# PSUM banks of the pairs' pools, the last W2 chunks of a pair, and the sixth row of a batch in a fused attention and ResMLP kernel

## The chip, the cores and the metric

The kernel runs on one core of one Trainium2 chip. The metric is the device time of one execution in microseconds; the time before is the median of three runs. All times inside a profile are counted from the start of the profiled span.

The engines are named as in the profile: PE is TensorE's matmul, PEld its weight load, DVE is VectorE, ACT is ScalarE, POOL is GpSimd, SP is SyncE. POOL and SP issue DMAs here. PSUM has eight banks; a bank holds 512 float32 values on each of 128 partitions, which is what one matmul of this kernel fills at most.

## The reference

```python
# attention: 8 batches, 16 query heads, 4 key/value heads, 384 tokens, head size 64
k = np.repeat(k, group, axis=1); v = np.repeat(v, group, axis=1)
scores = scale * np.matmul(q, k.transpose(0, 1, 3, 2))
attn = softmax(scores)
x = np.matmul(attn, v)             # laid out as [8, 384, 1024]
# ResMLP
a1 = alpha1 * x + beta1
tok = np.einsum('ts,bsd->btd', w_tok, a1)
u = x + lam * tok
a2 = alpha2 * u + beta2
ch = np.maximum(a2 @ w_ch1, 0.0) @ w_ch2    # 1024 -> 4096 -> 1024
out = u + lam * ch
```

Inputs and output are float32; the matmuls are done in bfloat16 with float32 sums.

## The kernel before

**Two streams, interleaved.** For each batch there is a "side" (attention and token mixing: everything up to a2) and a channel MLP. The channel MLP of batches 0 and 1 is done plainly (`main`). Batches 2 to 7 go in three pairs (`pair(i)`, i = 0, 1, 2), each by a scheme of the Strassen-Winograd kind with seven products for two batches. The generator of the channel MLP yields after each small piece of matmul work, and a plan written out by hand (`plan`) says which steps of which side run at which yield. So the order on every engine is fixed by the program text; it follows the order in which the instructions are issued.

**Stage 1 of a pair** has eight steps g = 0 to 7. A step has 14 groups of four matmuls of 384 columns (`SEQ1`, line 720): products o = 1 to 7 for two halves e of 128 hidden units. They are summed into PSUM tiles X (o = 1, 6, 5, 3), Y (o = 7, 4) and Z (o = 2), which ACT and DVE empty. The operands on the activation side are the tiles `opb(0)` to `opb(6)`: the transposed a2 of the two batches and sums of it. `sums_a(j)` (three DVE additions, lines 584 to 586) makes such sums for two rows of a2; one more, `opb(6)`, is made after the fourth group of g = 0 (line 737). `sum_w1(g, o)` makes W1's sums for step g on DVE (lines 619 and 624), and for g + 1 they are made during step g, the first of them (o = 5) after the third group.

**Stage 2 of a pair** has seven products, in the order o = 1, 2, 6, 5, 3, 7, 4 (`PLACE2`). Each has three row blocks ms = 0, 1, 2, and each of these 16 matmuls of 512 columns into a tile C (line 781). The work goes in pieces of four matmuls, called half blocks here, u = 0 to 83: after each the generator yields. The last product, o = 4, is done in two halves h = 0 and 1 with three tiles C open at once: ms = 0 and 1 in the pool "acc", ms = 2 in a tile of the pool "sc". Where a product is done, DVE adds it to an earlier one (line 818, for o = 7 line 820 too), scales it by lam (`scaled`, line 684, called a little later by `flush`), and POOL adds it into `out` in DRAM (`store`, line 515).

**The side in stage 2.** While stage 2 of pair i runs, the sides of both batches of the next pair run between its half blocks, the second 39 half blocks after the first. A batch has eight rows p = 0 to 7 (a row is two heads, 128 columns). For each row: scores and exponentials (`scores3`), then `av` (18 matmuls, line 314), after which DVE computes for this row rinv, xr, a1f and a (lines 319, 322, 327, 329); then `tok_flip`: `tok` (nine matmuls, line 339) with DVE's sum u (line 346) and a2 (line 350), the spill of u to `out` by SP (`spill`), and the transposition of a2. For the last three rows of the second batch this is done by PE (`turn`, three matmuls, line 426, and a copy by ACT), for all others by a DMA transpose on SP's queue. The tables of `side` give the half block of each step; `av` of rows 5, 6, 7 stands at 29, 33, 35, `tok_flip` at 34, 36, 38, `turn` at 37, 39, 41. With the shift by 39 the second batch's end falls into o = 4, whose half blocks are u = 72 to 83.

**PSUM in the pairs.** `share_banks` closes the pools of one stage and opens those of the next. Stage 1 has X (three tiles), Y (three) and Z (two), one bank each, in banks 0 to 2, 3 to 5, 6 and 7. Stage 2 has "sc" (three tiles of two banks each, banks 0 to 5), which serves the scores, av, tok and turn in rotation (`three`) and gives C of ms = 2 of o = 4 its tile, and "acc" (two tiles, banks 6 and 7) for all other C. A new pool over the banks of an old one waits for the old pool's last readers.

**Weights.** `w1` is a ring of six slots of 512 KB, for chunks of W1 (loaded and cast from DRAM on POOL's queue, `load_w1`, line 185) and, in stage 2, for the 28 chunks of W2's combinations (`fetch`, from the DRAM scratch `w2s` on SP's queue, line 635). `pad` has two more such slots; in stage 1 it holds W1's sums. `queue` lists loads in order; `pump` issues the head of it whenever a slot comes free (`free`). A step g of stage 1 needs the chunks g and g + 8, which are `order1[2g]` and `order1[2g+1]`. Four of them, for g = 0 and 1, are loaded ahead in stage 2 of the pair before (`heads`).

Of the kernel before, what the change touches and what calls it, by code (L numbers as in the profile page):

```python
# [12 lines left out]
def kernel(  # L13
# [22 lines left out]
    f32 = mybir.dt.float32  # L36
# [158 lines left out]

    def three():
        if pairs:
            return pairs["sc"].tile([P, 2, 4, P], f32, tag="sc", name="sc", bufs=3)
        return threes[0].tile([P, 2, 4, P], f32, tag="sc", name="sc", bufs=3)

    def one():
# [26 lines left out]
    def side(b):  # L228
# [201 lines left out]
        if not first:  # L430


            turns = {}
            if b == 1:
                turns = {4: [(to_all, 3, 0, 0), (to_all, 3, 1, 1), (load_row_set, 1, 1, 0), (load_row_set, 2, 0, 1)],
                         8: [(k_transpose, 0)], 12: [(to_all, 1, 0, 2), (to_all, 1, 1, 0), (load_row_set, 2, 1, 0)],
                         16: [(scale_beta,)], 20: [(to_all, 2, 0, 1), (to_all, 2, 1, 0)],
                         24: [(q_transpose, 0, 2, "av")], 28: [(k_transpose, 2)]}
                for i in range(3):
                    turns[32 + 4 * i] = [(q_transpose, 2 + 2 * i, 2, "av")]  # L440
            if (b - NPL) // 2 > 0:
                at = {}

                def put(k, *m):
                    at.setdefault(k, []).append(m)

                for j in range(6):
                    put((0, 6, 12, 21, 26, 31)[j], scores3, j, j in (2, 5))
                for p in range(NP):
                    put((4, 10, 14, 18, 24, 29, 33, 35)[p], av, p)  # L450
                    put((8, 15, 17, 22, 27, 34, 36, 38)[p], tok_flip, p)
                    if by_pe(p):
                        put((37, 39, 41)[p - NP + 3], turn, p)
                return turns, at
            return turns, {
                0: [(scores3, 0)], 4: [(av, 0)], 6: [(scores3, 1)], 8: [(tok_flip, 0)], 11: [(av, 1)],
                13: [(scores3, 2, True)], 15: [(av, 2)], 16: [(tok_flip, 1)], 18: [(tok_flip, 2)], 19: [(av, 3)],
                21: [(scores3, 3)], 23: [(tok_flip, 3)], 25: [(av, 4)], 27: [(scores3, 4)], 29: [(tok_flip, 4)],
                31: [(av, 5)], 33: [(scores3, 5, True)], 35: [(av, 6), (tok_flip, 5)], 37: [(av, 7)],
                38: [(tok_flip, 6)], 41: [(tok_flip, 7)],  # L460
                **{39 + 4 * i - i // 2 * 2: [(turn, p)] for i, p in enumerate((5, 6, 7)) if by_pe(p)}}
# [164 lines left out]
    NB = (B - NPL) // 2  # L626
    w2_slots, w2_at = {}, {}

    def padded(i, n):
        return n % 8 > 5 or i + 1 < NB and n >= SLOTS - 2  # L630

    def fetch(i, n):
        w2_slots[i, n] = slot = (pad_free if padded(i, n) else w1_free).pop(0)
        w2_at[i, n] = ring[:, slot] if slot < RING else pad[:, (slot - RING + 1) * 2048:(slot - RING + 2) * 2048]
        nc.sync.dma_start(out=w2_at[i, n], in_=w2s[n])

# [4 lines left out]
    def pump():  # L641
        while queue:
            f, *a = queue[0]
            if not (pad_free if f == fetch and padded(*a) else w1_free):
                return
            queue.pop(0)
            f(*a)
# [1 line left out]
    pad_free = []  # L649
    queue = []  # L650
    for i in range(NB):
        heads = [(load_w1, c) for c in order1[:4]] if i + 1 < NB else []
        queue += [(load_w1, c) for c in order1[4 if i else RING:]] + [(fetch, i, n) for n in range(SLOTS - 2)] + heads[:2]
        queue += [(fetch, i, n) for n in (SLOTS - 2, SLOTS - 1)] + heads[2:]

    IDENT = mybir.ActivationFunctionType.Identity
    SEQ1 = ((1, 0), (1, 1), (7, 0), (6, 0), (6, 1), (7, 1), (5, 0), (5, 1), (2, 0), (3, 0), (3, 1), (2, 1), (4, 0), (4, 1))
# [4 lines left out]

    def share_banks(*names):
        pair_banks.close()
        for name in names:
            pairs[name] = pair_banks.enter_context(tc.psum_pool(name=name, bufs=3))

    def pair(i):
        b0 = NPL + 2 * i
        share_banks("X", "Y", "Z")  # L670

        ends = {}

# [33 lines left out]
        for g in range(NH // 2):  # L707
            X, Y, snap = {}, {}, {}
            for k, (o, e) in enumerate(SEQ1):
                t = 2 * g + e  # L710
                lo, hi = bias1[:, t:t + 1], bias1[:, NH + t:NH + t + 1]
                if o == 1:
                    X[e] = pairs["X"].tile([P, 512], f32, tag="X", name="X", bufs=3)
                if o == 7:
                    Y[e] = pairs["Y"].tile([P, 512], f32, tag="Y", name="Y", bufs=3)
                if o == 2:
                    Z = pairs["Z"].tile([P, 512], f32, tag="Z", name="Z", bufs=2)
                ps = (X[e] if o in (1, 6, 5, 3) else Y[e] if o in (7, 4) else Z)[:, :S]
                for dt in range(NDT // 2):
                    nc.tensor.matmul(out=ps, lhsT=tb[g, o][:, dt, e * P:(e + 1) * P], rhs=opb(LEFT1[o])[:, dt],  # L720
                                     start=(o in (1, 2, 7) and dt == 0), stop=(dt == NDT // 2 - 1), skip_group_check=True)
                if o in (1, 6, 5):
                    q = ((2 if g % 2 else 8) + 2 * (1, 6, 5).index(o) + e) % 12 * S
                    snap[o, e] = snaps[:, q:q + S]
                    nc.scalar.activation(out=snap[o, e], in_=ps, func=IDENT, bias=hi if o == 5 else lo)  # L725
                if o == 5:
                    tt(out=hid[:, t, 1], in0=Y[e][:, :S], in1=snap[5, e], op=ADD)  # L727
                elif o == 2:
                    tt(out=hid[:, t, 0], in0=ps, in1=snap[1, e], op=ADD)
                elif o == 3:  # L730
                    nc.scalar.activation(out=hid[:, t, 4], in_=ps, func=RELU, bias=hi)
                elif o == 4:
                    tt(out=hid[:, t, 2], in0=ps, in1=snap[6, e], op=ADD)
                if (o, e) in ((2, 1), (3, 1)):
                    free(w1_slots.pop(g if o == 2 else g + NCH // 2))
                if k == 3 and g == 0:
                    tt(out=opb(6), in0=opb(4), in1=opb(5), op=SUB)
                if k == 2 and i and g == 0:
                    sum_w1(0, 4)
                if k in (2, 5, 8, 11) and g + 1 < NH // 2:  # L740
                    sum_w1(g + 1, {2: 5, 5: 7, 8: 6, 11: 4}[k])
                ts = slice(2 * g, 2 * g + 2)
                if k == 1 and g:
                    finish(slice(2 * g - 2, 2 * g))
                if (o, e) == (3, 1):
                    nc.scalar.activation(out=hid[:, ts, 1], in_=hid[:, ts, 1], func=RELU)
                if (o, e) == (4, 1):
                    nc.vector.tensor_scalar(out=hid[:, ts, 2], in0=hid[:, ts, 2], scalar1=0.0, scalar2=None,
                                            op0=mybir.AluOpType.max)
                    tt(out=hid[:, ts, 3], in0=hid[:, ts, 2], in1=hid[:, ts, 1], op=ADD)  # L750
                yield 0
        finish(slice(NH - 2, NH))
        share_banks("sc", "acc")
        acc = pairs["acc"]

        def c_banks(ms):
            return [(0, 512, pairs["sc"].tile([P, 2, 512], f32, tag="sc", name="C", bufs=3)[:, 0] if ms == NST - 1 else
                     acc.tile([P, 512], f32, tag="acc", name="C", bufs=2))]

        X = [c_banks(ms) if last else None for ms in range(NST)]  # L760
# [2 lines left out]
        for k, o in enumerate(PLACE2):  # L763
            whole = not last and o != 4
            for h in range(1 if whole else 2):
                for ms in range(NST):
# [2 lines left out]
                    if last and (o, h) in ((6, 1), (7, 0)):  # L769
                        (lift_end if o == 7 else begin_end)(ms)  # L770
                    if last and (o, h, ms) == (7, 0, NST - 1):
                        X[ms] = [(c0, c1, pairs["sc"].tile([P, 2, 512], f32, tag="sc", name="C", bufs=3)[:, 0, :c1 - c0])
                                 for c0, c1 in ((0, 384), (384, 512))]
                    if whole:
                        X[ms] = [(0, 512, acc.tile([P, 512], f32, tag="acc", name="C", bufs=2))]
                    elif not last and h == 0:
                        X[ms] = c_banks(ms)
                    upto = NH if whole else 8 * h + 8
                    for (c0, c1, x), t in ((c, t) for c in X[ms] for t in range(8 * h, upto)):
                        slot, rhs = w2_slots[i, 4 * k + t // 4], w2_at[i, 4 * k + t // 4]  # L780
# [49 lines left out]
    with tc.manual_schedule(engines=order):  # L830
# [162 lines left out]
        for i in range(NB - 1):  # L993
# [6 lines left out]
            for u, f, h in ((10, flip_q, 0), (17, flip_k, 0), (18, flip_q, 2), (28, flip_q, 4), (33, flip_k, 2), (33, flip_q, 6)):  # L1000
                put(ps, 1, u, f, c + 1, h, 2)
            put_all(ps, 1, side(c + 1)[1], lambda u: u + 39)
            for j, u in ((1, 78), (0, 78), (2, 80), (3, 82)):
                put(ps, 1, u, sums_a, j)
        for ps in range(NPL + NB):
            done = [0, 0]
# [7 lines left out]
            if ps == NPL - 1:  # L1014
                side_banks.close()
                mm_banks.close()
                pairs["open"] = True
            for key in [k for k in plan if k[0] == ps]:
                for f, *a in plan.pop(key):
                    f(*a)  # L1020
# [30 lines left out]
```

## Time and profile before

| | |
|---|---|
| runs | 755.1, 755.03, 754.49 us; median 755.03 |
| profiled execution | 752.46 us, its span 750.7 us, mean granted TensorE clock 0.997 |
| pair 0, stage 1 and stage 2 | 243.3 to 316.1, then X of pair 1 at 421.45 |
| pair 1, stage 1 and stage 2 | 421.45 to 496.0, then X of pair 2 at 601.30 |
| pair 2 | 601.30 to the end, 750.7 |

Below are PE's instructions around the end of pair 0's stage 2. The columns are the start, the time from the first start to the last end, engine, line, operation, output and input, the shape of a matmul, and how many run on end. Matmuls are pipelined, so the ends that are given overlap the next start; what a group costs is read from start to start.

```profile
403.62 1.03 PE L781 MATMUL C<-w,arena 128*128 128x512 bf16 x4
404.49 0.71 PE L314 MATMUL sc<-v,es 128*128 128x65 bf16 x18
405.04 1.02 PE L781 MATMUL C<-w,arena 128*128 128x512 bf16 x4
405.90 0.67 PE L339 MATMUL sc<-a,wtokT 128*128 128x128 bf16 x9
406.40 1.03 PE L781 MATMUL C<-w,arena 128*128 128x512 bf16 x3
```

The first line is the first half block of o = 4 (u = 72), the second is `av` of row 6, the fourth is `tok` of row 5. So a half block takes 404.49 - 403.62 = 0.87 us, an `av` 0.55 and a `tok` 0.50.

The DMAs that the change touches, from the page's list of issues (line, queue, count, KB each, median microseconds from issue to landing):

```profile
w<-in_moe_w_ch_dram POOLq DMA_DIRECT2D x68, 512.0 KB, 10.6
w<-w2s SPq DMA_DIRECT2D x62, 512.0 KB, 4.8
pad<-w2s SPq DMA_DIRECT2D x22, 512.0 KB, 8.2
```

### The profile page before, as it was taken

How to read it: one execution, taken by the hardware profiler on the slowest of the kernel's cores; microseconds unless marked ns; L12 is line 12 of the kernel's file. 1: busy time of each engine (PE TensorE's matmuls, PEld its weight loads, DVE VectorE, ACT ScalarE, POOL GpSimd, SP SyncE). 2: the span in 40 equal slices, each digit the busy share in tenths (PEclk: the TensorE clock that was granted, in tenths of full speed). 3: DMA queues.
4: the chain of work that ended last, by engine and by line, in shares of the span. 5: the costliest groups of instructions: out<-in, count | busy, mean ns of one | idle time of the engine just before them, and what ended most of it. 6: DMA issues, size and time to landing. Idle time of an engine off the chain costs nothing.

```text
span 750.7 us, 14462 instructions
## 1 busy us (share of the span) xinstructions
PE 729.8 (97%) x5710; PEld 419.1 (56%) x5769; DVE 521.3 (69%) x1010; ACT 318.7 (42%) x458; POOL 163.4 (22%) x211
## 2 busy tenths in 40 slices
PE   8999999999999999999999799999999899999997
PEld 5866555666555666555555466655555456654444
DVE  8763466578677899759678777748958977762344
ACT  7622431442432666644333366663343266660000
POOL 9434220520001330301023233200002322100011
PEclk9999999999999999999999999999999999999999
DMA  9999999999998999999979999989979998937975
GB/s 190 195 201 201 207 219 187 167 196 199 237 281 233 159 222 201 269 244 225 262 177 208 200 151 172 175 210 207 270 227 184 210 161 113 141 128 238 293 204 104
DMA packets 218018, 151.32 MB, mean 202 GB/s; under 512 B 88661, under 2 KB 197061, under 8 KB 217949
## 3 DMA queue, kind: packets, MB, share of 16 engines
q0 software_dynamic: 120304, 64.60, 65.4%
q1 hardware_dynamic: 97100, 85.39, 41.5%
q8 instruction: 45, 0.74, 0.4%
q10 hardware_dynamic: 544, 0.39, 0.2%
q14 instruction: 25, 0.20, 0.1%
HBM read 154.84 MB, written 38.27 MB: 257 GB/s over the span
## 4 chain that ended last, share of the span: by engine, by line
PE 86%; DVE 9%; DMA 2%; issue 2%; ACT 0%; DVEq 0%
PE C L781 23%; PE X L720 17%; PE h L530 10%; PE ch L568 10%; PE Y L720 8%; PE sc L278 4%; PE Z L720 4%; PE sc L314 3%; PE sc L339 3%; DMA pad<-w2s 1%; DMA ops<-a 1%; DVE xr L322 1%; DVE a1f L327 1%; DVE xr L346 1%; DVE hT L818 1%
## 5 line engine op out<-in xcount | busy, mean ns | idle before, releaser
L287 ACT ACTIVATE es<-sc 128x1024 bf16<-128x1024 f32 x126 | 121.4, 1023 | 163.9 <-PE sc L278 154.4
L781 PE MATMUL C<-w,arena 128*128 128x512 bf16 (+2 forms) x731 | 169.3, 372 | 1.7
L781 PEld LDWEIGHTS <-arena 128*128 128x128 bf16 x1040 | 94.8, 98 | 103.0 <-issue 8.0
L725 ACT ACTIVATE hT<-X,bias 128x384 f32<-128x384 f32 x144 | 83.6, 581 | 68.7 <-PE X L720 60.8
L720 PEld LDWEIGHTS <-w 128*128 128x128 bf16 x768 | 75.2, 98 | 57.2 <-issue 6.9
L185 POOL DMA_DIRECT2D w<-in_moe_w_ch_dram x68 | 61.0, 914 | 136.9 <-PE X L720 82.0
L568 PE MATMUL ch<-arena,hT 128*128 128x512 bf16 x366 | 87.9, 379 | 1.0 <-issue 0.3
L515 POOL DMA_DIRECT2D out_dram<-hT x33 | 28.5, 863 | 263.6 <-DVE hT L684 165.2
L530 PE MATMUL h<-ops,w 128*128 128x384 bf16 (+1 forms) x480 | 83.1, 327 | 0.8 <-DVE hT L541 0.7
L720 PEld LDWEIGHTS <-pad 128*128 128x128 bf16 x576 | 56.7, 98 | 37.9 <-issue 1.0
L720 PE MATMUL X<-ops,w 128*128 128x384 bf16 x384 | 70.6, 327 | 6.1 <-DVE hT L818 5.3
L720 PE MATMUL X<-ops,pad 128*128 128x384 bf16 x384 | 71.0, 328 | 0.0
L781 PE MATMUL C<-pad,arena 128*128 128x512 bf16 (+2 forms) x268 | 63.2, 373 | 2.8 <-DMA pad<-w2s 2.6
L530 PEld LDWEIGHTS <-w 128*128 128x128 bf16 x480 | 45.4, 98 | 30.2 <-issue 2.4
L568 PEld LDWEIGHTS <-hT 128*128 128x128 bf16 x384 | 34.7, 98 | 36.8 <-issue 2.5
L339 PEld LDWEIGHTS <-wtokT 128*128 128x128 bf16 x576 | 37.5, 98 | 13.9 <-DVE a L329 3.0
L314 PEld LDWEIGHTS <-es 128*128 128x128 bf16 x1008 | 38.3, 97 | 12.4
L727 DVE TENSOR_TENSOR arena<-Y,hT 128x384 bf16<-128x384 f32 x48 | 26.7, 557 | 24.1 <-ACT hT L725 21.8
L346 DVE TENSOR_TENSOR xr<-sc,xr 128x384 f32<-128x384 f32 x56 | 30.9, 551 | 18.1 <-PE sc L339 18.1
L278 PE MATMUL sc<-qT,kT 64*128 64x384 bf16 (+2 forms) x576 | 41.5, 271 | 1.6 <-ACT hT L287 0.3
L319 DVE RECIPROCAL rinv<-sc 128x6 f32<-128x6 f32 x56 | 10.7, 191 | 42.8 <-PE sc L314 42.7
L314 PE MATMUL sc<-v,es 128*128 128x65 bf16 x1008 | 39.9, 193 | 0.0
(138 smaller groups left out, 922.8 us busy)
## 6 DMA issues: line engine op xcount, KB each, us to landing
w<-in_moe_w_ch_dram POOLq DMA_DIRECT2D x68, 512.0 KB, 10.6
w<-w2s SPq DMA_DIRECT2D x62, 512.0 KB, 4.8
pad<-w2s SPq DMA_DIRECT2D x22, 512.0 KB, 8.2
out_dram<-xr SPq DMA_DIRECT2D x56, 192.0 KB, 6.8
out_dram<-hT POOLq DMA_DIRECT2D x33, 256.0 KB, 7.7
arena<-in_moe_w_ch_dram POOLq DMA_DIRECT2D x16, 512.0 KB, 20.0
w2s<-arena SPq DMA_DIRECT2D x28, 256.0 KB, 3.8
q_raw<-in_q_dram POOLq DMA_DIRECT2D x28, 192.0 KB, 10.5
```

Of the source, the lines that this page charges most:

```text
L185: nc.gpsimd.dma_start(out=w1[:, w1_slots[c]], in_=w1src[:, :, c * CW * P:(c + 1) * CW * P])
L278: nc.tensor.matmul(out=sc[:, hh, k % 4:k % 4 + n], lhsT=kT[r, 2 * p // G, BLK[hh][sk], :], rhs=qT[r, p, st:st + n, :], start=True, stop=True)
L287: nc.scalar.activation(out=e, in_=sc, func=EXP, scale=scale_qk)
L314: nc.tensor.matmul(out=av[:, hh, sq, :], lhsT=ess[k // 4][:, m % 2, k % 4, :], rhs=vb[:, sk, hk, :], start=(sk == 0), stop=(sk == NST - 1))
L339: nc.tensor.matmul(out=ps[:, tt, :], lhsT=wtokT[:, st, tt * P:(tt + 1) * P], rhs=a1s[p][:, st, :], start=(st == 0), stop=(st == NST - 1 an ...
L346: nc.vector.tensor_tensor(out=u, in0=ps, in1=u, op=ADD)
L515: nc.gpsimd.dma_start(out=at, in_=o, accum_op=ADD)
L530: nc.tensor.matmul(out=ps[:, :n], lhsT=w1[:, w1_slots[c], dt, j * P:(j + 1) * P], rhs=a2T[:, dt, :n], start=(dt == 0), stop=(dt == NDT - 1))
L568: nc.tensor.matmul(out=ps, lhsT=hT[:, nt, ms * P:(ms + 1) * P], rhs=w2[:, row(nt)[0], row(nt)[1], cs], start=(i == 0), stop=(i == NNT - 1))
L720: nc.tensor.matmul(out=ps, lhsT=tb[g, o][:, dt, e * P:(e + 1) * P], rhs=opb(LEFT1[o])[:, dt], start=(o in (1, 2, 7) and dt == 0), stop=(dt ...
L725: nc.scalar.activation(out=snap[o, e], in_=ps, func=IDENT, bias=hi if o == 5 else lo)
L781: nc.tensor.matmul(out=x, lhsT=hid[:, t, LEFT2[o], ms * P:(ms + 1) * P], rhs=rhs[:, t % 4 * 512 + c0:t % 4 * 512 + c1], start=((not last o ...
```

## The change

It has three parts.

*Banks.* Stage 1 opens its pools in the order Z, X, Y: Z gets four tiles (banks 0 to 3), X two (4 and 5), Y two (6 and 7). Stage 2 opens "acc" (banks 0 and 1) and three pools of one two-bank tile each, sc1 (2 and 3), sc0 (4 and 5) and sc2 (6 and 7). `three` takes them in turn by a counter and leaves out sc1 while C of ms = 2 of o = 4 lies there ("held").

*Chunks.* The last two W2 chunks of pairs 0 and 1 (n = 26 and 27) go to ring slots, not to `pad`, and are queued after the two W1 chunks of g = 0. Only these two W1 chunks stand ahead of them; the two of g = 1 come next, as slots come free. `pad_free` is emptied when a pair begins.

*Places.* For batches 4 and up `tok_flip` of row 5 is at half block 32 instead of 34, its `turn` at 36 instead of 37. `sums_a(1)` is at u = 77 and `sums_a(0)` at u = 74, both 78 before.

```diff
     def three():
         if pairs:
-            return pairs["sc"].tile([P, 2, 4, P], f32, tag="sc", name="sc", bufs=3)
+            pairs["turn"] = (pairs["turn"] + 1 + (pairs["turn"] == 0 and pairs["held"])) % 3
+            return pairs["sc%d" % pairs["turn"]].tile([P, 2, 4, P], f32, tag="sc", name="sc", bufs=1)
...
-                    put((8, 15, 17, 22, 27, 34, 36, 38)[p], tok_flip, p)
+                    put((8, 15, 17, 22, 27, 32, 36, 38)[p], tok_flip, p)
                     if by_pe(p):
-                        put((37, 39, 41)[p - NP + 3], turn, p)
+                        put((36, 39, 41)[p - NP + 3], turn, p)
...
-    def padded(i, n):
-        return n % 8 > 5 or i + 1 < NB and n >= SLOTS - 2
+    def padded(n):
+        return n % 8 > 5
...
     for i in range(NB):
-        heads = [(load_w1, c) for c in order1[:4]] if i + 1 < NB else []
-        queue += [(load_w1, c) for c in order1[4 if i else RING:]] + [(fetch, i, n) for n in range(SLOTS - 2)] + heads[:2]
-        queue += [(fetch, i, n) for n in (SLOTS - 2, SLOTS - 1)] + heads[2:]
+        heads = [(load_w1, c) for c in order1[:2]] if i + 1 < NB else []
+        queue += [(load_w1, c) for c in order1[2 if i else RING:]] + [(fetch, i, n) for n in range(SLOTS - 2)] + heads
+        queue += [(fetch, i, n) for n in (SLOTS - 2, SLOTS - 1)]
...
     def share_banks(*names):
         pair_banks.close()
+        pairs["turn"], pairs["held"] = 2, False
         for name in names:
-            pairs[name] = pair_banks.enter_context(tc.psum_pool(name=name, bufs=3))
+            pairs[name] = pair_banks.enter_context(tc.psum_pool(name=name, bufs=2))
 
     def pair(i):
         b0 = NPL + 2 * i
-        share_banks("X", "Y", "Z")
+        share_banks("Z", "X", "Y")
+        pad_free.clear()
...
-                    X[e] = pairs["X"].tile([P, 512], f32, tag="X", name="X", bufs=3)
+                    X[e] = pairs["X"].tile([P, 512], f32, tag="X", name="X", bufs=2)
                 if o == 7:
-                    Y[e] = pairs["Y"].tile([P, 512], f32, tag="Y", name="Y", bufs=3)
+                    Y[e] = pairs["Y"].tile([P, 512], f32, tag="Y", name="Y", bufs=2)
                 if o == 2:
-                    Z = pairs["Z"].tile([P, 512], f32, tag="Z", name="Z", bufs=2)
+                    Z = pairs["Z"].tile([P, 512], f32, tag="Z", name="Z", bufs=4)
...
-        share_banks("sc", "acc")
+        share_banks("acc", "sc1", "sc0", "sc2")
         acc = pairs["acc"]
 
         def c_banks(ms):
-            return [(0, 512, pairs["sc"].tile([P, 2, 512], f32, tag="sc", name="C", bufs=3)[:, 0] if ms == NST - 1 else
+            return [(0, 512, pairs["sc1"].tile([P, 2, 512], f32, tag="sc", name="C", bufs=1)[:, 0] if ms == NST - 1 else
                      acc.tile([P, 512], f32, tag="acc", name="C", bufs=2))]
...
                     elif not last and h == 0:
                         X[ms] = c_banks(ms)
+                        pairs["held"] = ms == NST - 1
...
-            for j, u in ((1, 78), (0, 78), (2, 80), (3, 82)):
+            for j, u in ((1, 77), (0, 74), (2, 80), (3, 82)):
                 put(ps, 1, u, sums_a, j)
```

The lines left out do the same for the last pair's two split C tiles (they take sc0 and sc2) and for the call of `padded`, and set the counter at the end of `main`. The change shifts line numbers: L781 before is L785 after, L720 is L723, L818 is L822, L684 is L687, L346 is L347, L624 is L625.

More of the change, by code (lines that the diff above doesn't have):

```diff
@@ L627 @@
     w2_slots, w2_at = {}, {}
-    def padded(i, n):
-        return n % 8 > 5 or i + 1 < NB and n >= SLOTS - 2
+    def padded(n):
+        return n % 8 > 5
     def fetch(i, n):
-        w2_slots[i, n] = slot = (pad_free if padded(i, n) else w1_free).pop(0)
+        w2_slots[i, n] = slot = (pad_free if padded(n) else w1_free).pop(0)
         w2_at[i, n] = ring[:, slot] if slot < RING else pad[:, (slot - RING + 1) * 2048:(slot - RING + 2) * 2048]
@@ L643, in pump @@
             f, *a = queue[0]
-            if not (pad_free if f == fetch and padded(*a) else w1_free):
+            if not (pad_free if f == fetch and padded(a[1]) else w1_free):
                 return
@@ L771, in pair @@
                     if last and (o, h, ms) == (7, 0, NST - 1):
-                        X[ms] = [(c0, c1, pairs["sc"].tile([P, 2, 512], f32, tag="sc", name="C", bufs=3)[:, 0, :c1 - c0])
-                                 for c0, c1 in ((0, 384), (384, 512))]
+                        X[ms] = [(c0, c1, pairs[sc].tile([P, 2, 512], f32, tag="sc", name="C", bufs=1)[:, 0, :c1 - c0])
+                                 for sc, c0, c1 in (("sc0", 0, 384), ("sc2", 384, 512))]
                     if whole:
@@ L1016 @@
                 mm_banks.close()
-                pairs["open"] = True
+                pairs["turn"] = 0
             for key in [k for k in plan if k[0] == ps]:
```

## The prediction

> **What bounds the kernel now.** I read the engines' shares, then TensorE's waits, then stretches by stage, then the timelines of TensorE (PE) and VectorE (DVE) in the last microseconds before a pair's stage 1. Times are in the 750.7 us span; the profiled execution took 752.46 us.
>
> ```profile
> PE 729.8 (97%) x5710; PEld 419.1 (56%) x5769; DVE 521.3 (69%) x1010; ACT 318.7 (42%) x458; POOL 163.4 (22%) x211
> ```
> ```profile
> PE X L720 <- DVE hT L818: 5.3, 2, 3.1
> PE C L781 <- DMA pad<-w2s: 2.6, 3, 1.8
> ...
> PE X L720 <- DVE obuf L575: 0.8, 1, 0.8
> ```
> PE is busy 97%, and the change adds or removes no instruction, so only PE's waits can move. Those of the pairs, 5.3 + 2.6 + 0.8 us (total, times, longest), are all this change can reach. They lie at three places: 0.8 where pair 0 begins, the rest where stage 2 of pairs 0 and 1 gives way to the next pair's stage 1.
>
> ```profile
> 414.53 1.89 PE L781 MATMUL C<-pad,arena 128*128 128x512 bf16 x8 [1.76 <-DMA pad<-w2s]
> ...
> 421.45 1.83 PE L720 MATMUL X<-ops,w 128*128 128x384 bf16 x8 [2.28 <-DVE hT L818]
> ```
> ```profile
> 601.30 1.46 PE L720 MATMUL X<-ops,w 128*128 128x384 bf16 x8 [3.06 <-DVE hT L818]
> ```
> So a transition has 1.76 + 2.28 us of idle (pair 0) or about 0.8 + 3.06 (pair 1). Start to start it is 17.83 us in both from the last half block of o=7 (403.62) to X (421.45); its work is 12 C half blocks of 0.864, three tok of 0.50, two av of 0.55, three turns of 0.165 (steps between starts) = 13.46, so 4.37 us is lost.
>
> ```profile
> 421.40:424.90 3.50, 3.45 (x14) 1.82 (x15) 3.31 (x5) 1.16 (x2) 1.63 (x2) 0.64 1.45 198
> ...
> 601.20:604.70 3.50, 3.40 (x21) 2.08 (x22) 3.35 (x5) 1.74 (x3) 0.84 (x1) 1.00 1.42 195
> ```
> The column after POOL's is the granted clock. After pair 0's transition PE ran part of this stretch at half clock and did 14 matmuls; after pair 1's, at 1.00, it did 21. From X to the first Z it took 428.33 - 421.45 = 6.88 us against 5.20: 1.68 us lost.
>
> **The change, part by part.**
>
> *X in other banks.* Before, X's pool begins in bank 0 and its release is pool-wide: it waits for the sum L818 of C of ms=2, which lies in a two-bank tile reaching into X's banks. After, X has banks 4 and 5; their last readers are older, so X follows the last C at once. At pair 0's start X likewise no longer waits for L575: -0.78 us; Y's sums there (L586, ending 244.15) are then needed near 244.3.
>
> *The wait that this makes.* C of ms=2 now takes bank 2, which tok of row 6 used in the half block before it. So it waits for DVE's L346 of that row. What is ahead of it there, from these rows:
>
> ```profile
> 408.57 0.19 DVE L319 RECIPROCAL rinv<-sc 128x6 f32<-128x6 f32 x1
> 408.80 0.56 DVE L322 TENSOR_TENSOR xr<-sc,rinv 128x384 f32<-128x384 f32 x1
> 409.39 0.56 DVE L327 TENSOR_TENSOR a1f<-xr,vecs 128x384 f32<-128x384 f32 x1
> 409.98 0.56 DVE L329 TENSOR_TENSOR a<-a1f,vecs 128x384 bf16<-128x384 f32 x1
> 410.46 0.55 DVE L346 TENSOR_TENSOR xr<-sc,xr 128x384 f32<-128x384 f32 x1
> ...
> 419.69 0.35 DVE L584 TENSOR_TENSOR ops<-ops 128x384 bf16<-128x384 bf16 x1
> 420.08 0.36 DVE L585 TENSOR_TENSOR ops<-ops 128x384 bf16<-128x384 bf16 x1
> 420.36 0.35 DVE L586 TENSOR_TENSOR ops<-ops 128x384 bf16<-128x384 bf16 x1
> 420.62 0.68 DVE L818 TENSOR_TENSOR hT<-C,hT 128x512 f32<-128x512 f32 x1
> ```
> Steps by starts: 0.22, 0.59, 0.59, 0.48 for a row's four; 0.59 for L346 and 0.47 for L350; 0.39 + 0.28 + 0.26 = 0.93 for a sums_a; 0.60 for L818, 0.72 with L684 behind it. PE after: C 403.62, av6 404.99, C, av7 407.27, C to 408.69, turn 5, tok6 408.85 to 409.35. DVE after: o=7's two sums and L684 from 403.82, with tok5's L346 and L350 between (row 5 is now earlier), then row 6's four, row 7's four from 408.1 (av7 ends 407.8), then sums_a(0), moved to this half block, at 410.46, and L346 of row 6 from 411.40 to 411.95. C of ms=2 starts at about 412.08: **2.73 us of idle where there was none.**
>
> *Then.* C of ms=2 to 413.81, tok7 to 414.31, h=1 of ms 0 and 1 with two turns to 418.08, ms=2 to 419.81; X at 419.81, not 421.45. What is late next is DVE: still two sums_a, three L818 and three L684 plus W1's first sum (L624, 0.60). The last L586 ends near 421.9; (7,0), third group of stage 1, needs it for its fourth matmul at 421.6: 0.44 us idle. Loss after: 2.73 + 0.44 = 3.17 against 4.37: **-1.2 us a transition, -2.4 for both.**
>
> *Two chunks into the ring.* The pad wait (1.76; about 0.8) goes. The two fetches issue at 400.6 to 402 when chunks 20 and 21 are read, not at 402.1 to 403.8. W1 of g=1 no longer loads beside them. They are read at 414.3 and 415.2. The fetch that PE waited for was issued at 402.1 and there at 414.5: 12.4 us, with the W1 loads beside it. By that slow row they land at 413.0 to 414.4, by the median of `pad<-w2s`, 8.2 us, at 408.8 to 410.2: cost 0 by either; were they 14 us on their way, 0.8.
>
> *W1 of g=1 later.* Its two loads used to issue at 402.14 and 403.05; now POOL waits with them until chunks 24 and 25 are read, about 413.4 and 414.3. Behind them in POOL's queue stand out_dram stores, which hold up nothing near. DVE's L624 of g=1, due at 424.0, waits for both; behind it is L737, needed by PE at 426.1 and ending 425.55. So a landing up to 424.45 is free. Landings took 5.9 and 8.5 us at 430.7 (two loads, queue otherwise idle), but 16.0 to 18.7 at 402 and 15.1 to 16.7 at 410.5 (four loads beside two fetches). I take the first pair, nearest in load: landing at 419.3 to 422.8, cost 0. The other end: 428.5 to 433, cost 4 to 8.5 a transition. W1 of g=2 is used eight us later and has room by either.
>
> *Y with two banks instead of three.* It then waits for L733 of the g before; by timeline the room is 13 ns at 262.6 and 289.9, 136 ns at 308.1, over 0.4 elsewhere. Cost 0 to 0.3, taken 0.15. X has 1.7 us of room.
>
> *Row 5 sooner.* Its spill and transpose pass flips of q and k in SP's queue, which have some 25 us of room: 0.
>
> *The clock.* Half clock came after 2.28 us of idle (pair 0), not after 3.06 (pair 1). The new 2.73 us stands between them, at both transitions. I assume one halving in two, as before: 0; bounds -1.7 (none) and +1.7 (both).
>
> The Trainium skill ("TensorE: Matmul & The Clock Gate", "Why this matters for your kernels") asks for no idle gaps over about 3 us, one idle window of 3.4 us bringing half clock. By it neither new gap would throttle, and the sum would be 1.7 us better. The trace's halving after 2.28 us says a shorter gap can do it, so I don't take this.
>
> **Sum:** -0.78 - 2.4 + 0.15 = -3.0 us: the profiled execution would take 749.4. The median of the runs, 755.03, is 2.6 us above it; I put the difference on the median: **752.0 us**.
>
> **The rivals.**
> - *More (no halving):* -3.0 - 1.7 = -4.7, 750.3; 748.6 if the timed runs had two before. For it: pair 1's gap of 3.06 did nothing. Against: the 2.28.
> - *Nothing to be measured:* halving in both, -1.3, and a row-6 wait longer by 0.5 each, -0.3: 753.7 to 754.7. For it: DVE, busy 17.1 of the 17.8 us, is the same before and after, so PE may only wait at another place.
> - *Slower (W1 of g=1 late):* DVE stops at L624, and PE at (3,0). It decides from a landing at 424.45 + 1.5 + 0.75 = 426.7, some 12.4 us after issue (1.5 us is the gain of a transition, 0.75 half the bound below). At 16 us it is 430.3, +5.85 a transition: -3.0 + 11.7, 763.7. For it: the rows at 402 and 410; against: those at 430.
> - *It doesn't do what it says:* if X's release still reached the sum of ms=2 (422.09 to 422.77 after, by the chain above), X would start at 422.85, 3.04 us after the last C; with the 2.73 that is 5.77 lost against 4.37: -0.78 + 2 x 1.4 + 0.15 = +2.2, 757.2. The new pools are separate, which speaks against it.
>
> **How the numbers follow.** Forecast 0.45, more 0.17, nothing 0.23, W1 late 0.12, not as it says 0.03. A measurement can tell 0.2%, 1.5 us: faster is under 753.5, slower over 756.5. The forecast and "more" are faster (0.62), "nothing" is same (0.23), the last two are slower (0.15). The range runs from 748.5 (no halving left, two before) to 757 (W1 landing 12.6 us after issue); beyond it lies most of the last two cases, some 0.12; the forecast's own range is 751 to 753.5.
>
> **What would show it.** Right: X L720 no longer follows L818 or L575; no wait for pad; C L781 (now L785) waits 2.7 us for xr L346 (L347) twice; Y waits about 0.4 for sums_a. Wrong: X or Y waiting for w, a C wait over 3.5, L624 held by a DMA, or granted clock 0.64 in both windows after X.

## The result and the profile after

The changed kernel takes 748.1 us (median of six runs, 746.87 to 750.17) against 754.76 for the kernel before beside it: ratio 0.9916, 95% interval 0.9896 to 0.9935. The profiled execution has a span of 745.6 us (747.4 us in all). The forecast was 752.0 with a range from 748.5 to 757: the sign was right, the gain, 6.7 us, is more than twice the 3.0 of the forecast, and the time lies just under the range.

PE's waits from pair 0's start to the last transition, in the changed kernel (total, times, longest):

```profile
PE C L785 <- DVE xr L347: 5.0, 2, 2.5
PE Y L723 <- DVE ops L586: 0.4, 2, 0.2
```

These two are all that is left. Gone are X's waits for L818 (5.3) and for the obuf sum L575 (0.8) and the wait for pad (2.6), as the prediction said. Gone too is one that it left out of its list. In the whole kernel before, the waits also had this line:

```profile
PE sc L339 <- DVE a L329: 1.2, 2, 0.6
```

Two waits of 0.6 us, one in each of pairs 0 and 1. The place is in the middle of stage 2, not at the transition; here is pair 0 before, PE and then DVE:

```profile
363.62 0.68 PE L339 MATMUL sc<-a,wtokT 128*128 128x128 bf16 x9 [0.60 <-DVE a L329]
```
```profile
359.94 0.55 DVE L346 TENSOR_TENSOR xr<-sc,xr 128x384 f32<-128x384 f32 x1
360.53 0.56 DVE L350 TENSOR_TENSOR obuf<-xr,vecs 128x384 bf16<-128x384 f32 x1
361.00 0.68 DVE L813 TENSOR_TENSOR hT<-C,hT 128x512 f32<-128x512 f32 x1
361.61 0.18 DVE L319 RECIPROCAL rinv<-sc 128x6 f32<-128x6 f32 x1
...
363.01 0.56 DVE L329 TENSOR_TENSOR a<-a1f,vecs 128x384 bf16<-128x384 f32 x1
```

This is the first batch of the next pair. DVE works without a gap: row 5's L346 and L350 (the first two lines), a C sum, then row 7's four operations, whose last ends 0.05 us before PE's tok of row 7 starts. With row 5 two half blocks sooner, DVE is done with it earlier and the wait is gone.

The transition of pair 0 in the changed kernel, PE:

```profile
403.57 0.67 PE L340 MATMUL sc<-a,wtokT 128*128 128x128 bf16 x9
...
408.80 0.67 PE L340 MATMUL sc<-a,wtokT 128*128 128x128 bf16 x9
411.94 1.89 PE L785 MATMUL C<-w,arena 128*128 128x512 bf16 x8 [2.48 <-DVE xr L347]
...
419.68 1.46 PE L723 MATMUL X<-ops,w 128*128 128x384 bf16 x8
420.98 0.65 PE L723 MATMUL Y<-ops,w 128*128 128x384 bf16 x3
421.82 0.32 PE L723 MATMUL Y<-ops,w 128*128 128x384 bf16 x1 [0.19 <-DVE ops L586]
```

The first line is tok of row 5, at the end of o = 7; the second is tok of row 6, whose bank C of ms = 2 takes next and waits for: 2.48 us (2.73 was forecast, with the start at 412.08). X follows the last C at 419.68 (419.81 forecast) with no wait. The fourth matmul of (7, 0) waits 0.19 (0.44 forecast). From the end of o = 7 to X it is now 419.68 - 403.57 = 16.11 us, against 17.83.

DVE's row that PE waits for, and what stands ahead of it:

```profile
410.40 0.35 DVE L585 TENSOR_TENSOR ops<-ops 128x384 bf16<-128x384 bf16 x1
410.79 0.36 DVE L586 TENSOR_TENSOR ops<-ops 128x384 bf16<-128x384 bf16 x1
411.07 0.35 DVE L587 TENSOR_TENSOR ops<-ops 128x384 bf16<-128x384 bf16 x1
411.34 0.55 DVE L347 TENSOR_TENSOR xr<-sc,xr 128x384 f32<-128x384 f32 x1
```

The clock after this wait, and in pair 1, in this execution (the column after POOL's is the granted clock):

```profile
411.90:415.40 3.50, 3.41 (x24) 1.93 (x25) 2.16 (x4) 0.00 (x1) 1.83 (x2) 1.00 0.31 65
588.10:591.60 3.50, 3.37 (x24) 1.93 (x25) 2.14 (x5) 0.00 (x0) 1.82 (x2) 1.00 0.98 231
```

Full clock at both. So the execution that was profiled has neither halving; the other runs, below, differ.

### The profile page after: what moved, and what is told of

The parts are those of the page before. It is cut to its first block, busy times and chain, and to the rows that moved or that the text cites. A ratio compares the mean times of both kernels' runs of the same rounds, so it can differ in the third digit from the quotient of the medians.

```text
span 745.6 us, 14462 instructions
## 1 busy us (share of the span) xinstructions
PE 728.5 (98%) x5710; PEld 418.7 (56%) x5769; DVE 522.2 (70%) x1010; ACT 319.1 (43%) x458; POOL 163.2 (22%) x211
## 4 chain that ended last, share of the span: by engine, by line
PE 85%; DVE 7%; DMA 4%; issue 2%; POOL 1%; ACT 0%; DVEq 0%
PE C L785 25%; PE X L723 16%; PE ch L569 10%; PE h L531 10%; PE Y L723 8%; PE sc L279 4%; PE Z L723 4%; PE sc L315 3%; PE sc L340 3%; DMA q_raw<-in_q_dram 2%; DMA ops<-a 1%; DVE xr L323 1%; DVE a1f L328 1%; DVE xr L347 1%; DVE hT L822 1%
## 5 line engine op out<-in xcount | busy, mean ns | idle before, releaser
L785 PE MATMUL C<-w,arena 128*128 128x512 bf16 (+2 forms) x777 | 179.8, 373 | 6.8 <-DVE xr L347 5.0
L785 PEld LDWEIGHTS <-arena 128*128 128x128 bf16 x1040 | 94.8, 98 | 105.7 <-issue 10.3
L723 PEld LDWEIGHTS <-w 128*128 128x128 bf16 x768 | 75.2, 98 | 50.0
L723 PEld LDWEIGHTS <-pad 128*128 128x128 bf16 x576 | 56.3, 98 | 38.0 <-issue 0.8
L723 PE MATMUL X<-ops,w 128*128 128x384 bf16 x384 | 70.3, 326 | 0.0
L723 PE MATMUL X<-ops,pad 128*128 128x384 bf16 x384 | 70.3, 326 | 0.0
L785 PE MATMUL C<-pad,arena 128*128 128x512 bf16 (+2 forms) x222 | 52.0, 372 | 0.1
L347 DVE TENSOR_TENSOR xr<-sc,xr 128x384 f32<-128x384 f32 x56 | 30.9, 552 | 21.3 <-PE sc L340 21.3
L723 PE MATMUL Y<-ops,w 128*128 128x384 bf16 x192 | 39.4, 326 | 0.4 <-DVE ops L586 0.4
L320 DVE RECIPROCAL rinv<-sc 128x6 f32<-128x6 f32 x56 | 10.7, 191 | 40.6 <-PE sc L315 40.5
```

Of the source, the lines that this page charges most:

```text
L347: nc.vector.tensor_tensor(out=u, in0=ps, in1=u, op=ADD)
L785: nc.tensor.matmul(out=x, lhsT=hid[:, t, LEFT2[o], ms * P:(ms + 1) * P], rhs=rhs[:, t % 4 * 512 + c0:t % 4 * 512 + c1], start=((not last o ...
```

## The experiments

**The kernel before once more, for its clocks (r0).** No edit.

> The kernel before, once more, to see the granted clock of each of its runs. If half-clock stretches explain what the changed kernel gained beyond its waits, the runs of 754 to 756 us have a mean granted clock near 0.995 (each stretch of 3.4 us at half clock takes 0.0023 off the mean and costs about 1.7 us) and the time falls by about 0.65 us for each 0.001 of clock. If the clock has nothing to do with it, all runs lie near 0.997 whatever their time. Ratio 1.000.

Measured: 754.96 us, ratio 0.9996 (0.998 to 1.0013). Over its 11 runs and the 51 of the kernel before that stood beside this and later runs, the mean granted clock is 0.9953 and the mean time 754.8. By clock: 756.2 us at 0.991 (2 runs), 756.6 at 0.993 (9), 755.0 at 0.995 (35), 753.6 at 0.997 (9), 753.8 at 0.998 (4), 751.5 at 0.999 (3); a straight line through all gives 0.64 us for each 0.001 and 751.8 at full clock. So the execution of before that was profiled for the prediction, at 0.997, was not a typical one. Every profiled execution at 0.997 in this document has one halved stretch, and those of the changed kernel at 0.995 (below) have two, so most runs of the kernel before have one more than that profile; none of them at 0.995 was profiled. This profile also shows that the pad wait was not what bound the transition:

```profile
421.76 1.81 PE L720 MATMUL X<-ops,w 128*128 128x384 bf16 x8 [4.21 <-DMA w<-in_moe_w_ch_dram]
```

Pair 0 had no pad wait here, and X waited 4.21 us instead of 2.28. It started 178.20 us after the X of pair 0, against 178.17 in the first profile: PE only waited at another place. The view names a DMA, but DVE's L818 began at 420.93 and X started 0.83 us later as in the first profile (420.62 to 421.45); the name is not to be trusted. DVE is busy nearly all the time in a transition; this is pair 0's in the first profile, from the end of o = 7 to X (DVE's is the third busy time, 17.11 of 17.83 us):

```profile
403.62:421.45 17.83, 13.69 (x119) 7.77 (x120) 17.11 (x38) 3.26 (x5) 5.09 (x6) 1.00 1.22 201
```

**Row 5 alone, in the kernel before (r1), and row 5 back, in the changed kernel (r2).** The edit of the first; the second takes the same step back.

```diff
-                    put((8, 15, 17, 22, 27, 34, 36, 38)[p], tok_flip, p)
+                    put((8, 15, 17, 22, 27, 32, 36, 38)[p], tok_flip, p)
                     if by_pe(p):
-                        put((37, 39, 41)[p - NP + 3], turn, p)
+                        put((36, 39, 41)[p - NP + 3], turn, p)
```

> The kernel before with only row 5 mixed two half blocks sooner and its turn one sooner. Theory A (DVE's backlog): DVE's sums of row 5 no longer stand ahead of row 7's a in the first batch of a pair, so the two waits of 0.60 us of tok L339 for a L329 go: 1.2 us faster, ratio 0.9984; the waits at the transitions stay. Theory B (my recorded prediction): row 5 is worth 0, ratio 1.000, and the waits of L339 stay.

> The changed kernel with row 5 back at its old places (34, and its turn at 37). Theory A: the two waits of L340 for L330 come back, 0.6 us each, so 1.2 us slower than the changed kernel: about 749.3 where that has 748.1, ratio to before 0.9927 to 0.993; the C wait at the transitions stays at about 2.5. Theory B: as the changed kernel, 0.9912.

Row 5 alone: 754.7 us, ratio 0.9987 (0.9975 to 0.9999), and no wait of L339 left in its profile: theory A, though the time alone could hardly tell it. Row 5 back: 744.82 us, ratio 0.9868 (0.9852 to 0.9883), 3 to 4 us *faster* than the changed kernel, which neither theory had: 1.6 us by its waits (3.8 against 5.4), the rest with its clock, 1.000 or 0.999 in its four runs. Its waits from pair 0's start to the last transition:

```profile
PE sc L340 <- DVE xr L347: 1.5, 2, 0.8
PE sc L340 <- DVE a L330: 1.2, 2, 0.6
PE Y L723 <- DVE ops L586: 1.1, 2, 0.5
```

The second line is what theory A said: the two waits come back. But the C wait of 2.5 is not there. With turn of row 5 behind C of ms = 2 again, one tile fewer is taken from the rotation ahead of C, so tok of row 6 lies in another tile; in its place tok of row 7 waits 0.75 us for a tile. So the three parts of the change are not additive: in the new banks, the earlier turn brings about the conflict.

**Without the conflict (r3).** The changed kernel with the rotation begun one place later.

```diff
-        pairs["turn"], pairs["held"] = 2, False
+        pairs["turn"], pairs["held"] = 0, False
```

> The changed kernel with the rotation of the three tiles begun one place later, so that tok of row 6 does not lie in the tile that C of ms=2 takes. Theory A (DVE bounds the transition): the C wait of 2.5 us goes, but DVE had only 1.3 us of idle time there, so Y's wait for the sums grows from 0.2 to about 1.5: 1.3 us less a transition, 2.6 in all, 745.5, ratio 0.988. Theory C (PE's wait is all that counts): 2.5 a transition, 5.0 in all, 743.1, ratio 0.985. Theory D (the wait only moves): 748.1, 0.991.

Measured: 744.01 us (743.83 to 744.84), ratio 0.9855 (0.9841 to 0.9868). The waits from pair 0's start to the last transition are one line:

```profile
PE Y L723 <- DVE ops L586: 2.5, 2, 1.2
```

PE no longer waits 2.5 us for C, and Y waits 1.23 us instead of 0.19. That is theory A to 0.3 us: L586 is the end of a chain on DVE, and taking away a wait on PE gains only what DVE had idle, here 1.4 us a transition where DVE's idle time behind the C wait was 1.29 in the changed kernel:

```profile
414.37 0.56 DVE L347 TENSOR_TENSOR xr<-sc,xr 128x384 f32<-128x384 f32 x1 [1.29 <-PE sc L340]
```

The time fell by more than these waits (2.9 us in both transitions), 4 to 5 us; the clock is 1.000 in three of its four runs and 0.999 in the other.

**Needless matmuls in the idle time (r4, r5).** In the changed kernel (r4) between tok of row 6 and C of ms = 2, in the kernel before (r5) between the last C and X; the core of the first:

```diff
+            if b > NPL + 1 and b % 2 and p == 6:
+                for _ in range(13):
+                    nc.tensor.matmul(out=full[:, 1, :NST].rearrange("p a d -> p (a d)"), lhsT=wtokT[:, 0, :P],
+                                     rhs=a1s[p].rearrange("p a d -> p (a d)"), start=True, stop=True)
```

> The changed kernel with 13 needless matmuls of 384 columns (0.163 us each, 2.1 us) in PE's idle time between tok of row 6 and C of ms=2, at both transitions. They wait for nothing and delay nothing. Theory E (half clock follows the idle time): the mean granted clock goes from 0.997 to 0.9995 or more and the time from 748.1 to about 746.2, ratio 0.9885, with the other waits of PE as they are. Theory F (only waits count, the clock is chance): clock 0.997, 748.1, ratio 0.991.

> The kernel before with the same 13 matmuls between the last C of a pair and the next X, where PE waits 2.2 to 4.2 us for L818. X starts when it did. Theory E: the clock goes from 0.995 to 0.998 or more and the time falls by 2 to 3.5 us, ratio 0.9955 to 0.9975, though no wait is shorter and there is more work. Theory F: ratio 1.000, clock 0.995.

In the changed kernel: 746.96 us, ratio 0.9894 (0.9874 to 0.9915), the clock 1.000 in all five runs, the C wait 0.65 instead of 2.48. In the kernel before: 752.18 us, ratio 0.9960 (0.9942 to 0.9978), the clock 1.000 in four runs of eight and 0.997 or 0.998 in the others. Its profiled execution, at 0.997, still has one stretch of half clock, behind the 2.08 us of idle time that the 13 matmuls leave ahead of X of pair 1:

```profile
421.90:425.40 3.50, 3.49 (x15) 1.87 (x16) 3.26 (x5) 1.16 (x2) 1.63 (x2) 0.66 1.35 203
```

Both go theory E's way: with more work and no wait ended sooner (in the changed kernel C even starts 0.29 us later after tok of row 6), both kernels run some 2 us faster. For the changed kernel the time alone would not settle it, since the interval overlaps the one without the matmuls; the clock does, 1.000 in five runs of five, where the 12 runs without them (six more are below) have 0.994 to 0.999. At clock 1.000 the medians are 747.0 and 751.2 (four runs), 4.3 us apart (3.9 by the means). With the 0.6 us by which C is late in the two transitions of the first, that is near the 5 us by which the waits differ.

**The banks of before, with all else of the change (r6).** The numbers of tiles and `three` are as before too.

```diff
-        share_banks("Z", "X", "Y")
+        share_banks("X", "Y", "Z")
...
-        share_banks("acc", "sc1", "sc0", "sc2")
+        share_banks("sc", "acc")
```

> The changed kernel with the banks and pools of before: only the ring change, row 5 and the sums' places are left. Theory A (DVE bounds the transition, the pad wait was hidden): the pad wait goes, but X then waits about 4 us for L822 and 0.8 for the obuf sum at pair 0's start; the ring change is worth 0 and the kernel runs as the one before with row 5 alone, 753.5 to 754.7, ratio 0.998 to 1.000. Theory G (the pad wait was worth its 1.8 and 0.8 us): 751.5, ratio 0.9955.

Measured: 754.18 us, ratio 0.9988 (0.9971 to 1.0006): theory A. The gain is in the banks; without them the rest is worth nothing that can be told by the time (its waits are 1.1 us less than before, which is row 5's, but its mean clock is 0.9936 where the kernel before has 0.9953). Its waits, and PE's clock behind both transitions:

```profile
PE X L722 <- DVE hT L821: 7.6, 2, 4.0
PE X L722 <- DVE obuf L575: 0.8, 1, 0.8
PE C L784 <- DMA w<-w2s: 0.4, 1, 0.4
```
```profile
421.50:425.00 3.50, 3.50 (x13) 1.77 (x14) 3.25 (x5) 1.16 (x2) 2.08 (x3) 0.56 1.27 160
600.80:604.30 3.50, 3.50 (x12) 1.60 (x13) 3.26 (x5) 1.16 (x2) 1.29 (x2) 0.50 1.37 196
```

The pad wait is gone and X's has grown from 5.3 to 7.6: 2.3 of the 2.6. And the two waits, gathered into one of 4.05 and one of 3.53 us, were each followed by half clock; behind the second it lasted some 6.8 us (599.4 to 606.3), and from X to the first Z took 7.88 us against 5.20.

**The ring change undone, in the changed kernel (r9).**

```diff
-        heads = [(load_w1, c) for c in order1[:2]] if i + 1 < NB else []
+        heads = [(load_w1, c) for c in order1[:4]] if i + 1 < NB else []
...
-        queue += [(fetch, i, n) for n in (SLOTS - 2, SLOTS - 1)]
+        queue += [(fetch, i, n) for n in (SLOTS - 2, SLOTS - 1)] + heads[2:]
```

`padded` is as before too.

> The changed kernel with the chunks and loads as before: the last two chunks of a pair in pad, four W1 chunks ahead. Theory A (DVE bounds the transition and hides the pad wait): the chunks are needed 2 to 3 us later than before, after the C wait of 2.5; at most 0.5 us of pad wait is seen a transition and Y's wait takes most of it up: 748.1 to 748.6, ratio 0.991 to 0.992. Theory G (the ring change was worth the pad wait, 2.6 us): 750.7, 0.995.

Measured: 749.19 us, ratio 0.9930 (0.9910 to 0.9950), with the same two waits as the changed kernel (5.0 and 0.4) and none for pad.

**The changed kernel once more, beside it (r11).** No edit.

> The changed kernel once more, beside the three others: ratio 0.9915, clock between 0.995 and 0.999 with a mean of 0.997, time falling by about 0.7 us for each 0.001 of clock. By waits alone it should be 4.9 us under the kernel before where both have the same clock.

Measured: 749.14 us, ratio 0.9930 (0.9908 to 0.9951). So the ring change is worth nothing here, by the time (749.19 against 749.14) and by the waits. This profile has the half clock that the first one of the changed kernel had not, behind the same wait:

```profile
411.08 3.31 PE L785 MATMUL C<-w,arena 128*128 128x512 bf16 x8 [2.48 <-DVE xr L347]
...
589.01 3.49 PE L785 MATMUL C<-w,arena 128*128 128x512 bf16 x8 [2.48 <-DVE xr L347]
```
```profile
411.00:414.50 3.50, 3.42 (x12) 1.39 (x12) 1.18 (x3) 0.00 (x0) 0.93 (x1) 0.55 0.19 56
588.90:592.40 3.50, 3.39 (x10) 1.20 (x10) 1.22 (x3) 0.00 (x0) 0.92 (x1) 0.52 0.72 170
```

Eight matmuls in 3.31 and 3.49 us instead of 1.89. The wait is 2.48 in this execution and in the first to the digit, so its length does not settle whether the clock is halved. Over both sets, 12 runs, the changed kernel has a mean clock of 0.9964 and a mean time of 748.8 us, and a line through them gives 0.62 us for each 0.001 and 746.6 at full clock.

**`sums_a(0)` back at u = 78 (r10).**

```diff
-            for j, u in ((1, 77), (0, 74), (2, 80), (3, 82)):
+            for j, u in ((1, 77), (0, 78), (2, 80), (3, 82)):
```

> The changed kernel with sums_a(0) back at u = 78, so 0.93 us less on DVE ahead of L347 of row 6. Theory A: the C wait falls from 2.48 to 1.55 us and Y's wait grows from 0.2 to about 1.1, so nothing is won by waits; but the longest idle time is shorter and half clock comes less often: clock 0.999, 746.5, ratio 0.989. Theory C (PE's wait is all that counts): 1.9 us by waits and the clock on top, 744.6, 0.9865.

Measured: 746.96 us, ratio 0.9901 (0.9883 to 0.9919), clock 1.000 in five runs of six. The waits:

```profile
PE C L785 <- DVE xr L347: 3.1, 2, 1.5
PE Y L723 <- DVE ops L586: 2.2, 2, 1.1
```

1.55 and 1.12 us each, as theory A had it: the sum, 5.3, is the same as 5.0 + 0.4. What 0.93 us less ahead of PE's wait gained by itself is nothing, and the 2.2 us against the changed kernel beside it (749.14) came with the clock.

**Two more steps along DVE's chain.** The kernel without the conflict, first with `sums_a(2)` and `sums_a(3)` sooner (r7), then with opb(6) sooner too (r8).

```diff
-            for j, u in ((1, 77), (0, 74), (2, 80), (3, 82)):
+            for j, u in ((1, 77), (0, 74), (2, 79), (3, 80)):
...
-                if k == 3 and g == 0:
+                if k == (1 if i else 3) and g == 0:
```

> The kernel r3_after_turn0 with the last two sums_a at u = 79 and 80 instead of 80 and 82, so that they stand ahead of the last sums L822 and scalings L687 on DVE. Theory A: Y's waits of 1.23 us go; the next thing late is opb(6), L740, by about 0.4 us at (3,0): 0.8 less a transition, 1.6 in all, 742.4, ratio 0.9834. Theory D (the wait only moves to opb(6) or to W1's sums): 744.0, 0.9855.

> r7_turn0_sums with opb(6) made two groups sooner, ahead of two of W1's sums on DVE. Theory A: X's waits of 0.77 us for L740 go; what is left in the transition is DVE's wait for W1 of g = 2 (3.1 us in r7, which cost PE 0.8): about 742.3, ratio 0.9835 to 0.9845. Theory D (the wait moves once more): 744 to 745, 0.986.

First step: 745.26 us, ratio 0.9861 (0.9839 to 0.9884). Y's wait of 1.23 is gone and X of (3, 0) waits 0.77 for L740 instead; in pair 1's stage 1 DVE then waits 3.1 us for W1 of g = 2, and Y 0.8 for DVE. No gain: theory D. Second step: 743.51 us (742.25 to 744.74), ratio 0.9855 (0.9831 to 0.9878). The wait for L740 is gone, and the profile has a wait of 0.96 us for a W2 chunk and three of Y, 0.3 each. Within the intervals it is no better than the one-line change of the rotation. In both steps a DMA landing is now among what is waited for; that these landings set the time is not shown.

## Why the prediction was half right

Its steps against what the profiles show, in us (two transitions together):

| step of the prediction | forecast | measured |
|---|---|---|
| X at pair 0's start without the wait for L575 | -0.78 | -0.8, no wait there |
| end of o = 7 to X | 2 x -1.64 | 2 x -1.72 (17.83 to 16.11) |
| (7, 0) waits for L586 | 2 x +0.44 | 2 x +0.19 |
| row 5 sooner | 0 | 2 x -0.60 |
| Y with two banks | +0.15 | 0, no such wait |
| clock | 0, bounds -1.7 and +1.7 | about -0.8 on 12 runs of the changed kernel |
| sum | -3.0 | -5.9 |

The mean times, 754.8 and 748.8, are 6.0 apart; at full clock the two lines are 5.2 apart, which leaves 0.8 for the clock. The spans of the two profiled executions, 750.7 and 745.6, are only 5.1 apart, though the first has a halving and the second none: in the second, X of pair 0 starts at 243.80 without a wait, where without its wait the first would have had it at 242.50. These 1.3 us lie ahead of the pairs and differ from one execution to the next: the second profile of the changed kernel has this X at 242.93.

**The transition was right**, in its mechanism and in its sizes: the wait that is removed, the new one and its place (2.48 for 2.73), X's start (0.13 us off), W1 of g = 1 landing in 5.9 and 8.6 us after issue (the row it chose said 5.9 and 8.5; in pair 1 it took 6.7 and 9.8), and what is late next. Of the rivals, the late W1 and the release that doesn't change did not occur, and no experiment made W1 of g = 1 late.

**The step "Row 5 sooner: 0" failed.** It counted the DMAs that row 5 moves past, and not DVE's work in the first batch, where the same tables hold. The line that would have shown it stood in the view of waits, between two lines that the prediction did quote, and was left out; "all this change can reach" was wrong. The runs with row 5 alone (r1) and with row 5 back (r2) show the 1.2 us go and come. The step failed on its other side too: the prediction had the new C wait and laid it to the banks, but did not see that it is the earlier turn of row 5 that puts tok of row 6 into the tile that C takes. With row 5 back there is no C wait, and the kernel is 3 to 4 us faster, the clock included.

**The term of the clock was mis-sized.** It took the one halving of one profiled execution as the kernel's habit, and put the 2.6 us by which the runs' median lay above that execution on both kernels alike. By their clocks, the kernel before mostly has two such stretches (0.995) and the changed kernel from none (0.999) to two (0.995). That the clock, not the waits, made this part of the time is shown by the needless matmuls: they take it away from the changed kernel in all five runs and from the kernel before in four of eight. Why the one set of six runs of the changed kernel has a mean of 0.9972 and the other 0.9957 stays open.

**The pad wait**, named as removed, was worth nothing by itself, as the prediction's sum from 4.37 to 3.17 implies but does not say: the run with the banks of before (r6) removes it and X waits longer, the one with the ring change undone (r9) restores its cause and no wait appears. The prediction also took the wrong fetch for the one that PE waited for: it was the one issued at 403.8, 10.7 us before C started, not the one at 402.1; the term was 0 either way. The version to take is the one with the rotation begun one place later (r3), 744.0 us: 0.6% under the changed kernel. There PE comes to these chunks sooner, and the ring change was not undone in it, so what it is worth there stays open.

## What to carry to other kernels

Where two engines take turns in waiting for each other, find the one with no idle time between; here it was DVE, busy 17.1 of 17.8 us. A wait removed from the other engine moves to the next place unless work leaves the busy one or is put in its idle time, and a wait's worth is found by that engine's gaps, not by its own length. When a kernel draws buffers from a rotation, moving any step across another use changes who meets whom: list the tiles by use after each move, as one step of the table here cost 3 to 4 us, the clock included, where it was taken to cost nothing. And read a change of a table at every place where the table is used.

## What the runs showed of the hardware

Half clock came behind waits of PE of 2.08, 2.24, 2.28, 3.53, 4.05 and 4.21 us, and behind 2.48 us in four cases of six. It did not come behind 2.25 us (twice) and 3.06 us, nor behind any wait of up to 1.76 us in these profiles. So the length of a wait between 2.1 and 3.1 us did not settle it, and what else does stays open. Kernels whose longest waits in the transitions were 1.55 us or less (1.55, 1.23, 0.96, 0.77, 0.75, 0.65) have a clock of 0.999 or 1.000 in all of their 28 runs. One such stretch of some 3.5 us cost 1.4 to 1.7 us, and the one of some 6.8 us cost 2.7. So breaking one wait of 2.5 into two of 1.55 and 1.12, with the same sum, made a kernel about 2 us faster, and so did filling most of it with needless matmuls.
